# A fused Fourier mixing and gated feed-forward kernel: one row of the opening spread by TensorE, four small stores on another queue, one weight fold inside the loop

## The chip, the cores and the metric

The kernel runs on one core of a Trainium2 chip. A core has five engines with queues of their own: TensorE (PE, with its weight loads as PEld), VectorE (DVE), ScalarE (ACT), GpSimd (POOL) and SyncE (SP), which issues most DMAs. An engine works through its own queue strictly in order. The metric is the device time of one execution in microseconds; lower is better.

## The reference

```python
X = np.fft.fft(x, axis=1)          # x: 8 x 3008 x 256, float32
X = np.fft.fft(X, axis=2)
x = X.real.reshape(24064, 256)
h = x @ w_in                       # 256 x 2048
g = h * np.cos(h)
out = g @ w_out                    # 2048 x 256
```

Each of the 8 batches is transformed along its sequence and along its channels; the real part goes through a two-layer feed-forward block with the activation h*cos(h).

## The kernel before

**The transform.** The sequence length 3008 is 47 times 64, and the transform is done in two halves. `fold` adds and subtracts mirrored channels of the input tile `xp`; `first_half` multiplies a chunk (eight chunks per batch) by the small constant `L` into PSUM tile `pz`; ScalarE copies it to `zs`. `store_z` writes `zs` to DRAM and `load_z` reads it back transposed as `z2`, because the second half needs another partition order. `second_half(b, g)` multiplies `z2` by the constant `BJ` into `pb`, and ScalarE copies that to `pq`. One call makes one of six groups of a batch: 225 columns for group 0, 256 for the others.

**The channel transform is folded into the weights.** `fold_weights(e, n)` multiplies the 512-column quarter n of `w_in` by the cosine (e=0, to `WC`) or sine matrix (e=1, to `WS`): two matmul calls per quarter and side, four matmul records in the trace (`pw`), and a copy out of PSUM. One channel, the middle one, has no sine part, so row 0 of `WS` would be multiplied by zeros; that row of weights is sent out through DRAM by `send_wn`, and comes back as a column by `load_wn` (tile `wn`). The row of data that belongs to it is row 0 of the second part of `pq`; it must lie on all 128 partitions as the tile `nb`. `seed` (line 525) then starts each PSUM tile `H` on ScalarE with `wn * nb + 0.25`.

**How `nb` is made.** For all groups but the first of batch 0, SP stores that row to DRAM (`nd`, line 383), and when it has landed reads it back to 128 partitions (`nb`, line 384). For group 0 of batch 0 `spread_nb` does it on the chip: a matmul of a column of ones with the row (line 391, `pn`), and a ScalarE copy (line 392).

**The main loop.** A step is one group times one of eight blocks of the hidden width (two halves, `units`), so there are 8 x 6 x 8 steps and twice as many units k. Per unit, TensorE multiplies with `WC` and `WS` (`mm1`, line 544; before the second product ScalarE reads the first, `act_e`, line 556), VectorE mirrors (line 560), ScalarE rounds (572), VectorE takes the fraction (576), ScalarE takes the sine (582), VectorE multiplies (586), and GpSimd forms three sums per step (`sums`, lines 602, 608, 609). Seven products with the recombined second weights (`mm2`, line 635) follow five units later. Units 0 to 15 belong to group 0, units 16 to 31 to group 1. Unit 16 is seeded during unit 15; this is the first use of the second `nb`.

**What sets the order.** All queues' orders are written out by hand (a manual schedule). Ahead of the loop come the eight chunks of batch 0, with the stores of the first 4 of 24 column blocks (chunks 0 to 5 by SP, 6 and 7 by ScalarE's queue), the weight folds of quarters 0, 1 and 2, and `second_half(0, 0)`. Quarter 3 is folded inside the loop at k = 0 and 1. The other work of the opening (the remaining stores and loads of z, the recombination of the second weights by GpSimd in `combine_w2`, `second_half` for groups 1 to 5) hangs on the table `opening`, by step; `second_half(0, 1)` stands at step 4, that is after unit 9. The next batch's input loads `load_x(1, p)` stand at steps 0, 2, 4 and 6 on SP's queue.

**DMA semaphores.** The program gives every DMA one of eight semaphores, in the order in which the DMAs are planned to issue; a DMA waits until the one before it on the same semaphore has landed. So a DMA can be held by one that has nothing to do with its data, and on ScalarE's queue such a wait holds all ScalarE work behind it.

**PSUM.** Eight banks: four for the tag M (`pz`, `pw`, the accumulators of `mm2`) and four, H0 to H3, that the units use in turn. `borrow` takes the H bank that the next seed will use, and does not advance the turn.

Of the kernel before, what the change touches and what calls it, by code (L numbers as in the profile page):

```python
# [82 lines left out]
def _width(g):  # L83
    return 225 if g == 0 else 256
# [24 lines left out]
def kernel(  # L109
# [7 lines left out]
    nc = tc.nc  # L117
# [46 lines left out]
    def raw(q, i):  # L164
        return wl[:, 512 * i : 512 * i + 512] if q == 3 else wr[i][:, 512 * q : 512 * q + 512]
# [22 lines left out]
    def load_w2(f0, f1):  # L188
        nc.sync.dma_start(
            out=w2.rearrange("p (q c) -> p q c", c=ND)[:, 2 * f0 : 2 * f1],  # L190
            in_=moe_w_out.rearrange("(q p) c -> p q c", p=128)[:, 2 * f0 : 2 * f1],
        )
# [17 lines left out]
    def psum(name, tag="H"):  # L210
        at = tag
        if tag == "H":
            at = f"H{turn[0] % 4}"
            turn[0] += 1
        return ppool.tile([128, 512], FP, tag=at, bufs=bank[tag], name=name)

    def borrow(name, k=0):
        return ppool.tile([128, 512], FP, tag=f"H{(turn[0] + k) % 4}", bufs=1, name=name)
# [110 lines left out]
    def store_z(b, c, j0=0, j1=NJ, eng=nc.sync):  # L329
        half, q = divmod(c, NCH // 2)  # L330
        if q == 0 and j0 == 0:
            zds[b, half] = dpool.tile([32, 2 * NJ * 128], FP, tag="zd", bufs=4, name="zd")
        zd, zs = zds[b, half], zss[b, c]
        for e in range(2):
            p0 = 16 * e + IP * q
            eng.dma_start(
                out=zd[p0 : p0 + IP, 256 * j0 : 256 * j1].rearrange("i (y d) -> y i d", d=128),
                in_=zs[64 * e + 2 * j0 : 64 * e + 2 * j1, :].rearrange("y (i d) -> y i d", d=128),
            )
# [11 lines left out]
    ready = {}  # L351

    def second_half(b, g):

        T = _width(g)
        z2 = z2s[b]
        pb = borrow("pb") if b or g else psum("pb", "M")
        for q in range(4):
            jj = 4 * g + q
            nc.tensor.matmul(  # L360
                pb[:, 128 * q : 128 * q + 128],
                lhsT=z2[:, jj * 128 : jj * 128 + 128],
                rhs=BJ[:, jj * 128 : jj * 128 + 128],
                start=q == 0,
                stop=True,
                skip_group_check=True,
            )
        pq = spool.tile([128, 512], FP, tag="pq", bufs=8, name="pq")
        pv = pq[:, 0 : 2 * T].rearrange("d (e t) -> d e t", e=2)
        bv = pb.rearrange("d (q e k) -> d e q k", q=4, e=2)  # L370
        if g == 0:
            nc.scalar.copy(
                out=pv[:, :, 0:192].rearrange("d e (q k) -> d e q k", k=64), in_=bv[:, :, 1:4, :]
            )
            nc.scalar.copy(out=pv[:, :, 192:225], in_=bv[:, :, 0, 0:33])
        else:
            nc.scalar.copy(out=pv.rearrange("d e (q k) -> d e q k", k=64), in_=bv)
        nb = spool.tile([128, 256], FP, tag="nb", bufs=8, name="nb")
        ready[b, g] = (pq, nb)
        if b == 0 and g == 0:  # L380
            return
        nd = dpool.tile([1, 256], FP, tag="nd", bufs=4, name="nd")
        nc.sync.dma_start(out=nd[:, 0:T], in_=pq[0:1, T : 2 * T])
        nc.sync.dma_start(out=nb[:, 0:T], in_=nd[0:1, 0:T].to_broadcast([128, T]))


    def spread_nb():
        pq, nb = ready[0, 0]
        T = _width(0)
        pn = psum("pn", "M")  # L390
        nc.tensor.matmul(pn[:, 0:T], lhsT=ones, rhs=pq[0:1, T : 2 * T], start=True, stop=True)
        nc.scalar.copy(out=nb[:, 0:T], in_=pn[:, 0:T])

# [27 lines left out]
    def fold_weights(e, n, tag="M"):  # L421
        keep_weights(e, n, weights(e, n, tag))

    def weights(e, n, tag="M"):
        pw = psum("pw", tag)
        for i in range(2):
            nc.tensor.matmul(  # L427
                pw,
                lhsT=CS[i][:, 128 * e : 128 * e + 128],
                rhs=raw(n, i),  # L430
                start=(i == 0),
                stop=(i == 1),
            )
        return pw

    def keep_weights(e, n, pw, copy=nc.scalar.copy):
        W = WS if e else WC
        copy(out=W[:, 512 * n : 512 * n + 512], in_=pw)
# [26 lines left out]
    def send_wn(n):  # L465
        row = WS[0:1, 512 * n : 512 * n + 512]
        wds[n] = dpool.tile([1, 512], FP, tag="wd", bufs=3, name="wd")
        nc.scalar.dma_start(out=wds[n], in_=row)
        nc.gpsimd.memset(row, 0.0)
# [331 lines left out]
    first_half(0, 4)  # L801
    chunk(6)
    first_half(0, 5)
    store_z(0, 4, 0, 4)
    store_z(0, 5, 0, 4)
    load_z(0, 0, 0, 4)
    chunk(7)
    first_half(0, 6)
# [1 line left out]
    first_half(0, 7)  # L810
    store_z(0, 7, 0, 4, nc.scalar)
    load_z(0, 1, 0, 4)
    for n in (1, 2):
        fold_weights(1, n)
        send_wn(n)
        fold_weights(0, n)
    load_w2(0, 2)
    load_w(3)
    load_w2(2, 4)
# [5 lines left out]
    for half in range(2):  # L825
# [5 lines left out]
        0: ((combine_w2, 0, 2), (combine_w2, 2, 4)),  # L831
        3: ((combine_w2, 4, 6, 0, 2),),
        4: ((combine_w2, 4, 6, 2, 4), (second_half, 0, 1)),
        5: ((combine_w2, 6, 8, 0, 2),),
        6: ((combine_w2, 6, 8, 2, 4),),
        10: ((second_half, 0, 2), (load_ident,)),
        14: ((second_half, 0, 3),),
# [10 lines left out]
    n = len(steps)  # L848
# [16 lines left out]
    for k in range(2 * n + LAG):  # L865
        t, u = divmod(k, 2)
        d, v = divmod(k - LAG, 2)
        cur, prev, old, nxt = unit(k), unit(k - 1), unit(k - 2), unit(k + 1)
        done = step(d)
        full = step(d if v else d - 1, True)  # L870
        if cur:
            if k % (2 * per) == 0:
                todo = transform(cur.s.b + 1) if cur.s.b + 1 < NB else {}
            if k >= AHEAD:
                mm1(cur, 0)
                act_e(cur)
            if k == 0:
                for h in (cur, nxt):
                    mm1(h, 0)
                    seed_first(h)  # L880
                    act_e(h)
                spread_nb()
            if k < AHEAD - 1:
                mm1(cur, 1)
            if k == 0:
                pw = [weights(1, 3)]
        pair = None if u else pairs.pop(t, None)
        if pair:
            b, c = pair
            pz = [first_half(b, c, borrow("pz"))]  # L890
        if old:
            dve_g(old)
            if old.u:
                sums(old.s)
        if pair:
            pz.append(first_half(b, c + 1, borrow("pz", 1)))
        pm = clear_middle() if u and t in middles else None
        if done:
            order = (0, 1, 5, 4, 3, 2, 6) if done is steps[-1] else range(7)
            mm2(done, 4 * v, 4 * v + 3, order)  # L900
        if pm is not None:
            middle(pm)
        if full and full is not steps[-1]:
            take_m(full, 1 if v else 3, nc.vector)
        if nxt and 0 < k < AHEAD - 1:
            seed(nxt)
        if prev:
            act_round(prev)
        if pm is not None:
            nc.scalar.copy(out=zm[64:128], in_=pm)  # L910
        if pair:
            keep_z(b, c, pz[0])
        if nxt and k >= AHEAD - 1:
            seed(nxt)
        if full and full is not steps[-1]:
            take_m(full, 0 if v else 2, nc.scalar)
        if prev:
            dve_frac(prev)
        if k + 1 in range(2, AHEAD):
            mm1(nxt, 0)  # L920
            act_e(nxt)
        if k == 1:
            pw.append(weights(0, 3))
        copy_small()
        if prev:
            act_sin(prev)
        if pair:
            keep_z(b, c + 1, pz[1])
            patch_z(b, c)
            patch_z(b, c + 1)  # L930
        if cur and k >= AHEAD - 1:
            mm1(cur, 1)
        if done and v == 0:
            mm2(done, 3, 4, order)
        if cur:
            dve_h(cur)
        if k in (1, 2):
            keep_weights(2 - k, 3, pw[k - 1], nc.vector.tensor_copy)
        elif k == 3:
            send_wn(3)  # L940
        elif k == 6:
            load_wn(3, nc.scalar)
        if u == 0:
            continue
        for i in range(6):
            s = step(t - 4 - i, True)
            if s:
                combine_m(s, i)
        for sg, lag in ((0, 8), (1, 10)):
            s = step(t - lag, True)  # L950
            if s:
                store_out(s, sg)
        for call in opening.pop(t, ()):
            call[0](*call[1:])
        for call in todo.pop(t % per, ()):
            call[0](*call[1:])
# [31 lines left out]
```

## Time and profile before

| | |
|---|---|
| three runs, us | 1957.72, 1954.21, 1953.16 (median 1954.21) |
| the profiled execution, us | 1952.79 |
| its span from first to last instruction, us | 1951.0 |
| mean granted TensorE clock | 0.999 |
| TensorE busy | 1935.9 us, 9232 matmuls |
| ScalarE, VectorE, GpSimd busy | 1508.9, 1457.7, 1400.2 us |

Times in the profile count from the span's start. A row of the timeline gives start, duration, engine, line, operation and tiles, and in brackets how long the engine was idle before it and what ended the idle time. PEld is the weight load that goes ahead of each matmul; SPq and ACTq are DMA issues on those queues, and such a row shows the issue alone and not the transfer. Matmuls overlap, so the duration of a row is longer than the distance to the next; the distances between starts are what TensorE costs.

### The profile page before, as it was taken

The page shows a single profiled execution, that of the slowest core. Times are in us where ns is not written, and L with a number is a line of the kernel's source. Part 1 is how long each engine was busy: PE and PEld are TensorE (multiplying, and loading weights), DVE is VectorE, ACT ScalarE, POOL GpSimd, SP SyncE. Part 2 cuts the span into 40 slices and gives each one's busy share as a digit, 9 for nine tenths or more (in the row PEclk, how much of TensorE's full clock was granted, in tenths as well). Part 3 has the DMA queues.
Part 4 walks back from the last instruction along what each step waited for, and adds up shares of the span by engine and source line. Part 5 has one row for each costly group of instructions (what it writes and reads, how often), then busy time and mean ns, then how long its engine had stood idle before and what let it go on. Part 6 is the DMA issues. An engine that isn't in the chain of part 4 may idle for free.

```text
span 1951.0 us, 29624 instructions
## 1 busy us (share of the span) xinstructions
PE 1935.9 (99%) x9232; PEld 1682.9 (86%) x9232; DVE 1457.7 (75%) x2531; ACT 1508.9 (77%) x3444; POOL 1400.2 (72%) x1594
## 2 busy tenths in 40 slices
PE   8999999999999999999999999999999999999998
PEld 4888899888988889888898888988889888898887
DVE  3667777777777777777777777777777777778787
ACT  3777778777787777877778787787777887778775
POOL 3777767787677876787668776687767777666765
PEclk9999999999999999999999999999999999999999
DMA  7712024111230112301241111411124121110001
GB/s 184 141 27 44 20 47 84 24 36 33 53 71 18 40 40 59 54 20 40 43 78 31 32 34 41 86 24 39 24 42 84 24 40 28 39 22 16 11 14 31
DMA packets 178280, 88.71 MB, mean 45 GB/s; under 512 B 104890, under 2 KB 175209, under 8 KB 176492
## 3 DMA queue, kind: packets, MB, share of 16 engines
q1 hardware_dynamic: 176582, 86.35, 21.7%
q8 instruction: 75, 1.23, 0.3%
q14 instruction: 81, 0.66, 0.1%
q10 hardware_dynamic: 1542, 0.47, 0.1%
HBM read 49.51 MB, written 37.28 MB: 44 GB/s over the span
## 4 chain that ended last, share of the span: by engine, by line
PE 98%; DMA 1%; ACT 0%; DVE 0%; SPq 0%; issue 0%; POOL 0%; POOLq 0%; DVEq 0%
PE M L635 58%; PE H L544 33%; PE pz L269 3%; PE pb L360 2%; PE pw L427 1%; DMA xp<-in_x_dram 0%; DMA wr<-in_moe_w_in_dram 0%; DMA nb<-nd 0%; DMA nd<-pq 0%; PE pz L266 0%; PE pm L317 0%; DVE r L576 0%; DVE cb L703 0%; ACT r L582 0%; POOL xf L252 0%
## 5 line engine op out<-in xcount | busy, mean ns | idle before, releaser
L602 POOL TENSOR_TENSOR S<-r 128x512 f32<-128x512 f32 (+1 forms) x383 | 475.6, 1242 | 447.1 <-DVE r L586 398.5
L576 DVE SCALAR_TENSOR_TENSOR r<-r,H 128x512 f32<-128x512 f32 (+1 forms) x768 | 518.3, 675 | 195.5 <-ACT r L572 168.7
L582 ACT ACTIVATE r<-r 128x512 f32<-128x512 f32 (+1 forms) x768 | 477.0, 621 | 240.1 <-DVE r L576 235.2
L586 DVE SCALAR_TENSOR_TENSOR r<-H,r 128x512 f32<-128x512 f32 (+1 forms) x768 | 518.9, 676 | 133.8 <-ACT r L582 93.9
L635 PE MATMUL M<-S,VX 128*128 128x256 f32 (+1 forms) x2304 | 616.0, 376 | 0.0
L635 PEld LDWEIGHTS M<-S,VX 128*128 128x128 f32 x2304 | 436.0, 190 | 71.5 <-issue 22.7
L544 PE MATMUL H<-pq,WC 128*128 128x256 f32 (+1 forms) x1536 | 454.0, 377 | 3.9 <-ACT H L525 3.9
L544 PE MATMUL H<-pq,WS 128*128 128x256 f32 (+1 forms) x1536 | 451.1, 375 | 1.0 <-ACT ew L556 1.0
L572 ACT ACTIVATE r<-H 128x512 f32<-128x512 f32 (+1 forms) x768 | 447.7, 583 | 0.2 <-DVE H L560 0.2
L560 DVE TENSOR_TENSOR H<-ew,H 128x256 f32<-128x256 f32 (+1 forms) x768 | 324.7, 423 | 142.5 <-PE H L544 83.6
L635 PE MATMUL M<-r,w 128*128 128x256 f32 (+1 forms) x1536 | 387.6, 375 | 0.0
L556 ACT ACTIVATE ew<-H 128x256 f32<-128x256 f32 (+1 forms) x768 | 287.9, 375 | 121.5 <-PE H L544 117.0
L525 ACT ACTIVATE H<-nb,wn 128x256 f32<-128x256 f32 (+1 forms) x766 | 366.0, 478 | 4.9 <-DMA nb<-nd 4.0
L635 PEld LDWEIGHTS M<-r,w 128*128 128x128 f32 x1536 | 300.5, 196 | 26.9
L544 PEld LDWEIGHTS H<-pq,WC 128*128 128x128 f32 x1536 | 279.3, 190 | 48.3 <-ACT H L525 13.1
L544 PEld LDWEIGHTS H<-pq,WS 128*128 128x128 f32 x1536 | 290.0, 190 | 34.7 <-issue 1.6
L608 POOL TENSOR_TENSOR S<-S,r 128x256 f32<-128x256 f32 (+1 forms) x383 | 276.0, 721 | 30.0
L609 POOL TENSOR_TENSOR S<-r,S 128x256 f32<-128x256 f32 (+1 forms) x383 | 275.2, 718 | 30.0
L635 PE MATMUL M<-S,w 128*128 128x256 f32 (+1 forms) x768 | 225.5, 375 | 0.0
L635 PE MATMUL M<-r,VX 128*128 128x256 f32 (+1 forms) x768 | 225.2, 375 | 0.0
L635 PEld LDWEIGHTS M<-S,w 128*128 128x128 f32 x768 | 150.8, 197 | 14.6
L635 PEld LDWEIGHTS M<-r,VX 128*128 128x128 f32 x768 | 145.8, 190 | 14.6
(78 smaller groups left out, 918.1 us busy)
## 6 DMA issues: line engine op xcount, KB each, us to landing
out_dram<-ob SPq DMA_DIRECT2D x724, 32.0 KB
xp<-in_x_dram SPq DMA_DIRECT2D x56, 256.0 KB
zd<-zs SPq DMA_DIRECT2D x112, 96.0 KB
z<-zd SPq DMA_DIRECT2D x28, 384.0 KB
xp<-in_x_dram SPq DMA_DIRECT2D x56, 120.0 KB
nb<-nd SPq DMA_DIRECT2D x40, 128.0 KB
wr<-in_moe_w_in_dram SPq DMA_DIRECT2D x8, 256.0 KB
w<-in_moe_w_out_dram SPq DMA_DIRECT2D x4, 512.0 KB
```

The costliest lines, as they stand in the source:

```text
L525: nc.scalar.activation(out=h.H[:, 0:T], in_=s.nb[:, 0:T], func=AF.Copy, bias=0.25, scale=wn[:, f : f + 1])
L544: nc.tensor.matmul(h.H[:, 0:T], lhsT=W[:, 128 * f : 128 * f + 128], rhs=s.pq[:, e * T : e * T + T], start=False, stop=True, skip_group_che ...
L556: nc.scalar.mul(out=h.ew[:, 0:T], in_=h.H[:, 0:T], mul=2.0)
L560: nc.vector.tensor_tensor(out=h.H[:, T : 2 * T][:, ::-1], in0=h.ew[:, 0:T], in1=h.H[:, 0:T], op=ALU.subtract)
L572: nc.scalar.activation(out=r, in_=y, func=AF.Copy, bias=BIG, scale=1.0)
L576: nc.vector.scalar_tensor_tensor(out=r, in0=r, scalar=-BIG, in1=y, op0=ALU.add, op1=ALU.subtract)
L582: nc.scalar.activation(out=r, in_=r, func=AF.Sin, bias=0.0, scale=SIN_SCALE)
L586: nc.vector.scalar_tensor_tensor(out=r, in0=y, scalar=-0.25, in1=r, op0=ALU.add, op1=ALU.mult)
L602: tt(out=sv[:, 0:2], in0=qv[:, 1:2].to_broadcast([128, 2, T]), in1=qv[:, 0:4:3], op=ALU.subtract,)
L608: tt(out=sv[:, 2], in0=sv[:, 1], in1=gv[:, 0, 0], op=ALU.subtract)
L609: tt(out=sv[:, 3], in0=gv[:, 1, 0], in1=sv[:, 2], op=ALU.add)
L635: nc.tensor.matmul(acc[key][m // 2][:, 256 * (m % 2) : 256 * (m % 2) + T], lhsT=w, rhs=a, start=first, stop=s.fp == 7, skip_group_check=True,)
```

## The change

Three things are moved in the opening of the kernel; nothing is changed from batch 1 on.

1. Group 1 of batch 0 gets its `nb` from `spread_nb(1)` instead of the two DMAs. It stands in `opening` at step 5 (after unit 11), and takes its PSUM tile by `borrow`.
2. The stores of chunks 4 and 5 (two DMAs each, first 4 column blocks) are issued by ScalarE's queue instead of SP's.
3. `fold_weights(0, 2)` is no longer done before `second_half(0, 0)`. Its matmuls come at k = 2 in the loop, after quarter 3's, and its copy out of PSUM is done by VectorE at k = 3.

```diff
-        if b == 0 and g == 0:
+        if b == 0 and g < 2:
             return
         nd = dpool.tile([1, 256], FP, tag="nd", bufs=4, name="nd")
         nc.sync.dma_start(out=nd[:, 0:T], in_=pq[0:1, T : 2 * T])
         nc.sync.dma_start(out=nb[:, 0:T], in_=nd[0:1, 0:T].to_broadcast([128, T]))
 
-    def spread_nb():
-        pq, nb = ready[0, 0]
-        T = _width(0)
-        pn = psum("pn", "M")
+    def spread_nb(g):
+        pq, nb = ready[0, g]
+        T = _width(g)
+        pn = borrow("pn") if g else psum("pn", "M")
         nc.tensor.matmul(pn[:, 0:T], lhsT=ones, rhs=pq[0:1, T : 2 * T], start=True, stop=True)
         nc.scalar.copy(out=nb[:, 0:T], in_=pn[:, 0:T])
...
     first_half(0, 5)
-    store_z(0, 4, 0, 4)
-    store_z(0, 5, 0, 4)
+    store_z(0, 4, 0, 4, nc.scalar)
+    store_z(0, 5, 0, 4, nc.scalar)
     load_z(0, 0, 0, 4)
...
-    for n in (1, 2):
-        fold_weights(1, n)
-        send_wn(n)
-        fold_weights(0, n)
+    fold_weights(1, 1)
+    send_wn(1)
+    fold_weights(0, 1)
+    fold_weights(1, 2)
+    send_wn(2)
...
-        5: ((combine_w2, 6, 8, 0, 2),),
+        5: ((combine_w2, 6, 8, 0, 2), (spread_nb, 1)),
...
-                spread_nb()
+                spread_nb(0)
...
-        if k == 1:
-            pw.append(weights(0, 3))
+        if k in (1, 2):
+            pw.append(weights(0, 4 - k))
...
-        if k in (1, 2):
-            keep_weights(2 - k, 3, pw[k - 1], nc.vector.tensor_copy)
-        elif k == 3:
+        if k in (1, 2, 3):
+            e, q = ((1, 3), (0, 3), (0, 2))[k - 1]
+            keep_weights(e, q, pw[k - 1], nc.vector.tensor_copy)
+        if k == 3:
             send_wn(3)
```

## The prediction

> **What bounds the kernel now.** I read the page first, then the chain of waits over the opening, then waits and stages around its longest break, because the change touches the opening alone.
>
> ```profile
> span 1951.0 us, 29624 instructions
> ...
> PE 98%; DMA 1%; ACT 0%; DVE 0%; SPq 0%; issue 0%; POOL 0%; POOLq 0%; DVEq 0%
> ```
>
> TensorE is on the chain for 98% of the span, so a gain is either TensorE work removed or TensorE idle time removed. The change removes no matmul (it adds two records, below); it can gain only in the part that is not TensorE. The chain shows where that is:
>
> ```profile
> 68.11 2.89 DMA nd<-pq
> 71.01 4.16 DMA nb<-nd
> 75.19 0.49 ACT H L525
> 75.72 1.22 PE H L544 x2
> ```
>
> ```profile
> ACT H L525 <- DMA nb<-nd: 4.0, 1, 4.0
> PE H L544 <- ACT H L525: 3.5, 1, 3.5
> ```
>
> The columns of the chain are start, duration, what. The two DMAs take 7.05 us; ScalarE idles 4.0 us for the second before it can seed unit 16, and TensorE 3.5 us behind it. The stages show a second loss: TensorE restarts at a lower granted clock (1.00 in every 4 us stage from 20 to 72).
>
> ```profile
> 72.00:76.00 4.00, 0.52 (x3) 0.28 (x2) 0.30 (x1) 0.81 (x2) 3.84 (x5) 0.93 0.87 147
> 76.00:80.00 4.00, 4.00 (x14) 3.53 (x15) 1.70 (x4) 2.16 (x8) 1.43 (x2) 0.64 1.06 159
> ```
>
> Columns: stage, busy time of PE, PEld, DVE, ACT, POOL, then clock, DMA share, GB/s. The clock is 0.64 in the 4 us after the idle stage.
>
> **Part 1: the row spread by TensorE.** What the wait costs is read from three equal places of the TensorE timeline, the first `WC` product of units 13, 15 and 17:
>
> ```profile
> 65.61 0.54 PE L544 MATMUL H<-pq,WC 128*128 128x225 f32 x2
> ...
> 69.80 0.54 PE L544 MATMUL H<-pq,WC 128*128 128x225 f32 x2
> ...
> 79.36 0.59 PE L544 MATMUL H<-pq,WC 128*128 128x256 f32 x2
> ```
>
> Two undisturbed units take 69.80-65.61 = 4.19 us, the two with the wait 79.36-69.80 = 9.56. The difference is 5.37, less 0.1 for the two products of unit 16 that are 256 instead of 225 columns wide (0.54 against 0.59 us in these rows): **5.27 us**, of which 3.5 are idle and 1.8 the slower matmuls. The lower bound is 3.5, if the low clock had another cause and stayed; I take 5.27, because no other stage shows it. The Trainium skill, "TensorE: Matmul & The Clock Gate", Part 1, says that an idle window of about 3.4 us drops the clock to half and that about 3.4 us of work restores it; this trace agrees (3.5 idle, 0.64 after).
>
> In its place come two matmul records and one ScalarE copy. Their price, and whether they wait:
>
> ```profile
> 38.02 0.38 PE pn L391 x2
> ...
> 62.23 0.62 DVE L586 SCALAR_TENSOR_TENSOR r<-H,r 128x450 f32<-128x450 f32 x1 [0.28 <-ACT r L582]
> ...
> 63.71 0.54 PE L544 MATMUL H<-pq,WC 128*128 128x225 f32 x2
> ...
> 60.00:64.00 4.00, 4.00 (x22) 3.83 (x22) 2.62 (x5) 3.30 (x9) 3.77 (x6) 1.00 1.06 302
> ```
>
> The 225-column spread cost TensorE 0.38 us; 256 columns make 0.38*256/225 = 0.43. It goes ahead of unit 12's `WC` product at 63.71. The borrowed bank was unit 9's, last read by the VectorE row that ends at 62.85, so TensorE does not wait for it. TensorE is busy 4.00 of 4.00 there, so 0.43 is paid in full. The copy sits behind unit 10's sine on ScalarE, which has 0.70 us free in that stage against about 0.4; behind it are unit 12's `act_e` and unit 13's seed, and both wait for TensorE's 0.43 anyway. Its result is wanted three units later: hidden. SP loses two issues, and the four loads that stood behind `nb` on its queue go some 3 us earlier (from behind 71.01 to about 68.1). Part 1: 0.43-5.27 = **-4.84**.
>
> **Part 2: stores by ScalarE's queue, and the fold taken out.** They go together: the fold hides the arrival of z.
>
> ```profile
> 21.86 8.08 SPq L336 DMA_DIRECT2D zd<-zs  x12
> 30.11 1.87 SPq L346 DMA_DIRECT2D z<-zd  x4
> 32.51 3.79 SPq L177 DMA_DIRECT2D wr<-in_moe_w_in_dram  x2
> ...
> 25.48 1.08 SPq L336 DMA_DIRECT2D zd<-zs  x2
> ```
>
> ```profile
> SPq L177 <- DMA wd<-WS: 2.9, 1, 2.9
> SPq L336 <- DMA wr<-in_moe_w_in_dram: 1.9, 2, 1.0
> ```
>
> ```profile
> 25.58 0.59 ACT L295 COPY zs<-pz 128x512 f32<-128x512 f32 x1 [2.01 <-PE pz L283]
> ...
> 27.75 0.63 ACTq L336 DMA_DIRECT2D zd<-zs  x2
> ```
>
> ```profile
> 26.67 7.13 PE L427 MATMUL pw<-wr,CS 128*128 128x512 f32 x16
> ...
> 33.67 0.97 PEld L360 LDWEIGHTS pb<-BJ,z 128*128 128x128 f32 x8 [0.70 <-issue]
> ...
> 39.73 0.30 PEld L427 LDWEIGHTS pw<-wr,CS 128*128 128x128 f32 x2 [0.72 <-DMA wr<-in_moe_w_in_dram]
> ...
> 28.00:32.00 4.00, 4.00 (x11) 1.79 (x10) 0.00 (x0) 1.17 (x2) 0.52 (x1) 1.00 0.28 61
> ```
>
> Sixteen fold records run from 26.67; at 0.43 each, four less end 1.72 us sooner, near 31.95. But the weight load of `pb` starts at 33.67 after 0.70 us, so z lands about then, some 2 us after SP's last of four issues (30.11+1.87 = 31.98, its start near 31.6). With z unmoved nothing is gained. SP now issues eight stores instead of twelve. The fourth store can't leave before 25.48 (held by a weight load, 1.9 us in two such waits); the last then leaves near 27.0, lands near 28.5 (I estimate 1.5 us for the landing of a store: before, the last of the twelve leaves near 29.65 and the third z load, which needs it, near 31.2, in the middle of its row), and the loads of the first half follow. Those of the second half need chunk 7's store, which ScalarE issues at 27.75 to 28.38; I add 0.2 for its four more issues (0.3 each, inside the 2.01 us idle before 25.58, except that the last is held by the same weight load until about 25.9). Landing 1.5 later, the last load leaves near 30.4 instead of 31.6: z comes **1.2 us** sooner (bounds: 0, if another landing holds it; 1.72, the fold). ScalarE's later copies wait for TensorE in any case. The DMA share of 0.28 says that the transfers have room.
>
> A side effect: SP's second load of quarter 3 was held 2.9 us by a landing of `wd` only because both used one semaphore. In the new order its predecessor is a z load that has landed by then, so quarter 3 arrives up to 2.9 us earlier, and TensorE, there 1.2 us sooner, doesn't wait for it (0.72 before).
>
> **Part 3: the fold put in at k = 2.**
>
> ```profile
> 41.62 1.72 PE pw L427 x4
> ...
> 44.54 0.65 PE L544 MATMUL H<-pq,WS 128*128 128x225 f32 x2 [0.45 <-ACT ew L556]
> 45.35 0.65 PE L544 MATMUL H<-pq,WC 128*128 128x225 f32 x2 [0.16 <-ACT H L525]
> ...
> 46.54 0.62 PE L544 MATMUL H<-pq,WS 128*128 128x225 f32 x2 [0.54 <-ACT ew L556]
> 47.42 0.65 PE L544 MATMUL H<-pq,WC 128*128 128x225 f32 x2 [0.27 <-ACT H L525]
> ...
> 46.03 0.36 ACT L556 ACTIVATE ew<-H 128x225 f32<-128x225 f32 x1 [0.27 <-PE H L544]
> ```
>
> It costs 1.72 us on TensorE, in front of four waits of 0.45+0.16+0.54+0.27 = 1.42. So the bounds are 0.30 and 1.72. Followed through: the product at 44.54 moves to 45.8 and the next, now without wait, to 46.2; it ends near 46.7, so the `act_e` at 46.03 starts 0.7 later, and all that hangs on it on ScalarE (sine, seed) with it: 47.42 becomes about 48.07. I take **+0.65**. VectorE's copy (0.7 us as its two neighbours) comes after the mirror of unit 3, where VectorE waits for ScalarE's late sine.
>
> **The sum.** -4.84-1.2+0.65 = **-5.4**. Against the profiled execution (1952.79 = span 1951.0 and 1.8 around it) that is 1947.4; the median of the runs lies 1.4 above that execution, and I forecast on its level: 1954.21-5.4 = **1948.8 us**. About 0.2% (3.9 us) is what can be told from no change.
>
> **The rivals.**
>
> *Nothing is gained ahead of the loop.* Z lands no sooner and the fold is paid in full at k = 2: 0+1.72-4.84 = -3.1, 1951.1. For it: ScalarE's DMAs use the same semaphores and can be held by the same weight loads. Against it: SP's twelve issues take 8.08 us at a DMA share of 0.28. The Trainium skill, "DMA: Bandwidth & Descriptors", section "Issuing engines are not separate DMA queues", speaks for this rival: all queues end on the same 16 engines, and a second issuing engine saves only issue time. No row here separates the two.
>
> *GpSimd takes the place of the removed wait.*
>
> ```profile
> 73.67 1.06 POOL L602 TENSOR_TENSOR S<-r 128x450 f32<-128x450 f32 x1
> ...
> 81.36 0.54 PE L635 MATMUL M<-S,VX 128*128 128x225 f32 x2
> ```
>
> Its sums of step 6 started at 73.67, while TensorE stood, and are first used at 81.36; 5.4 us sooner that is 75.96, against 74.73, when they are there. The margin is 1.2 us; GpSimd was busy 3.77 and 3.84 of 4.00 us around there. Were its queue 3 us later (its recombinations wait for loads of the second weights), TensorE would lose 1.8: 1950.6. Against it: those loads move forward with SP's queue.
>
> *Slower: ScalarE is held by a DMA semaphore.* Its send and load of quarter 3's row take new semaphores, and now follow other stores.
>
> ```profile
> 52.34 0.40 ACTq L472 DMA_DIRECT2D wn<-wd  x1
> ...
> SPq L150 <- DMA wn<-wd: 4.3, 1, 4.3
> ...
> 59.30 0.32 SPq L150 DMA_DIRECT2D xp<-in_x_dram  x1
> ```
>
> A DMA of this stretch can be in flight from 52.34 to 59.30, 7 us. If ScalarE had to wait for one as long, TensorE would stand about 7 us and restart slowly (1.8 as above): -5.4+7+1.8 = +3.4, 1957.6. It decides from a hold of 3.6 us with the slow restart. Against it: both follow stores issued some 5 us before, as they did.
>
> **How the numbers follow.** Forecast 0.70 (its own range 1947.3 to 1950.4: the bounds of z's arrival and of part 3), nothing gained ahead of the loop 0.15, GpSimd 0.08, ScalarE held 0.07. Two in ten are left out by 1946.5 to 1953.0, where the two middle rivals lie with the runs' spread. Faster by over 0.2% (below 1950.3): nearly all of the forecast and a part of the middle two, 0.73. Slower by over 0.2% is ScalarE held, with a part of it inside the bound and other unseen holds, 0.07. Within 0.2%: 0.20.
>
> **What would show it.** Right: no wait of line 525 for `nb` near 70 us and a clock of 1.00 there; `pb`'s first weight load near 32.5; the first product behind the new fold follows without idle time; unit 17's `WC` product near 73.9 instead of 79.36. Wrong: TensorE idle time in front of `pb` as long as the fold that left, an idle ScalarE behind one of its DMA issues, or products with `S` that wait for GpSimd.

## The result, and the profile after

The changed kernel takes 1947.69 us (median of 7 executions, 1947.33 to 1948.46); the kernel before, run beside it, 1954.21 us (7 executions, 1952.76 to 1958.42). The ratio is 0.9959 with a 95% interval of 0.9949 to 0.9970: faster by 0.4%, or 8.0 us (5.9 to 10.0). The medians alone differ by 6.5 us, the two profiled executions by 5.5 (1952.79 and 1947.33). Forecast were -5.4 us and 1948.8 us. The three measured differences do not agree, because the executions of before spread over 5.7 us and those of the changed kernel over 1.1; what spreads them is half of this study.

The page of the changed kernel:

```profile
span 1945.5 us, 29626 instructions
...
PE 98%; DMA 1%; SPq 0%; DVE 0%; issue 0%; ACT 0%; DVEq 0%
```

The same stages as in the prediction (duration, busy time of PE, PEld, DVE, ACT, POOL, clock, DMA share, GB/s), and the new product of the changed kernel with the first `WC` products of units 15 and 17, which answer to the rows at 69.80 and 79.36:

```profile
72.00:76.00 4.00, 4.00 (x22) 3.77 (x21) 3.05 (x6) 3.29 (x11) 3.84 (x6) 1.00 1.10 169
76.00:80.00 4.00, 4.00 (x22) 3.71 (x21) 3.06 (x6) 3.60 (x9) 2.34 (x4) 1.00 0.89 150
```

```profile
62.61 0.69 PE L391 MATMUL pn<-pq,ones 1*128 1x256 f32 x2
...
69.43 0.54 PE L544 MATMUL H<-pq,WC 128*128 128x225 f32 x2
...
73.72 0.59 PE L544 MATMUL H<-pq,WC 128*128 128x256 f32 x2
```

TensorE is busy 4.00 of 4.00 in both stages, the clock is 1.00, and unit 17's first product comes at 73.72 instead of 79.36.

The gain can be cut into stretches that begin where TensorE starts a row that both kernels have: the first fold record, and the three first calls of `second_half`. After (and, behind it, the two rows of before that the prediction did not show):

```profile
26.26 5.42 PE L427 MATMUL pw<-wr,CS 128*128 128x512 f32 x12
32.27 1.13 PE L360 MATMUL pb<-BJ,z 128*128 128x128 f32 x8 [0.59 <-DMA z<-zd]
...
57.36 1.05 PE L360 MATMUL pb<-BJ,z 128*128 128x128 f32 x8
...
85.14 1.05 PE L360 MATMUL pb<-BJ,z 128*128 128x128 f32 x8
```

```profile
58.56 1.05 PE L360 MATMUL pb<-BJ,z 128*128 128x128 f32 x8
...
90.78 1.05 PE L360 MATMUL pb<-BJ,z 128*128 128x128 f32 x8
```

Every kernel below is cut the same way, each in its own profiled execution, in us. The first `pb` of before starts at 33.70.

| kernel | first fold | fold to 1st pb | 1st to 2nd pb | 2nd to 3rd pb | to the span's end |
|---|---|---|---|---|---|
| before | 26.67 | 7.03 | 24.86 | 32.22 | 1860.2 |
| changed | 26.26 | 6.01 | 25.09 | 27.78 | 1860.4 |
| row_only | 27.46 | 7.27 | 24.69 | 27.77 | 1860.0 |
| row_and_stores | 27.77 | 6.97 | 24.61 | 27.92 | 1859.9 |
| row_and_fold | 27.69 | 7.22 | 25.09 | 28.74 | 1860.4 |
| stores_fold_only | 26.83 | 5.95 | 25.09 | 34.79 | 1860.5 |
| before_again | 27.38 | 7.13 | 25.90 | 36.48 | 1860.2 |
| wait_kept_warm | 27.11 | 7.18 | 24.69 | 30.64 | 1860.2 |
| before_bj_late | 27.32 | 7.21 | 24.70 | 28.01 | 1860.3 |
| before_bj_early | 26.23 | 7.11 | 24.82 | 33.75 | 1860.2 |
| after_bj_late | 27.81 | 5.92 | 25.09 | 27.78 | 1860.4 |
| before_wn_on_chip | 27.00 | 7.16 | 24.84 | 30.35 | 1860.0 |
| after_wn_on_chip | 27.44 | 6.14 | 25.42 | 27.77 | 1860.4 |

The last column is the same in all to 0.6 us: whatever any edit does happens before the third `pb`. The first column does not go by the edits: it lies between 26.26 and 27.81 in the kernels with the stores moved and between 26.23 and 27.69 in the others. I take it for chance between executions, 0.41 us of it in favour of the changed kernel's profile. What the edits do is in the three columns between.

### The profile page after: what moved, and what is told of

Same layout as the page of the kernel before. It is cut to its first block, busy times and chain, and to the rows that moved or that the text cites. A ratio compares the mean times of both kernels' runs of the same rounds, so it can differ in the third digit from the quotient of the medians.

```text
span 1945.5 us, 29626 instructions
## 1 busy us (share of the span) xinstructions
PE 1933.3 (99%) x9234; PEld 1681.4 (86%) x9234; DVE 1459.1 (75%) x2532; ACT 1508.3 (78%) x3444; POOL 1400.4 (72%) x1594
## 4 chain that ended last, share of the span: by engine, by line
PE 98%; DMA 1%; SPq 0%; DVE 0%; issue 0%; ACT 0%; DVEq 0%
PE M L635 59%; PE H L544 34%; PE pz L269 3%; PE pb L360 2%; DMA xp<-in_x_dram 1%; DMA wr<-in_moe_w_in_dram 0%; PE pw L427 0%; DMA zd<-zs 0%; PE pz L266 0%; PE pm L317 0%; DMA z<-zd 0%; DVE cb L703 0%; SPq L147 0%; PE H L531 0%; PE po L733 0%
```

## The experiments

All medians are of the runs that the ratio compares; each group of kernels was timed beside executions of before of its own (medians 1955.85 for row_only, stores_fold_only, wait_kept_warm and before_again; 1956.66 for row_and_fold, before_bj_late, before_bj_early and after_bj_late; 1954.29 for row_and_stores, before_wn_on_chip and after_wn_on_chip).

### Which part does what

**row_only**: part 1 of the change alone.

```diff
-        if b == 0 and g == 0:
+        if b == 0 and g < 2:
...
-        5: ((combine_w2, 6, 8, 0, 2),),
+        5: ((combine_w2, 6, 8, 0, 2), (spread_nb, 1)),
```

> The kernel before with part 1 alone: the second group's row is spread by TensorE; stores and fold stay as they were. Theory (the forecast's step): the wait of 5.27 us goes and 0.43 comes, so about 4.8 us under the profiled execution of before, near 1948.0; since the executions of before lie between 1952.8 and 1958.4 and those of the changed kernel between 1947.3 and 1948.5, I expect the spread of before to go with this part too, and the ratio near 0.996. Rival (the spread comes from the opening ahead of the loop): near 1948 with single executions 4 to 5 us above.

Measured: 1948.96 us, ratio 0.9967 (0.9955 to 0.9980). Part 1 brings most of the gain. Its effect is all in the stretch from the second to the third `pb`: 32.22 becomes 27.77, that is -4.45. The executions lie between 1948.07 and 1951.25: narrower than before's but not as narrow as the changed kernel's.

**stores_fold_only**: parts 2 and 3 alone (the changed kernel with the row again through DRAM).

```diff
-        if b == 0 and g < 2:
+        if b == 0 and g == 0:
...
-        5: ((combine_w2, 6, 8, 0, 2), (spread_nb, 1)),
+        5: ((combine_w2, 6, 8, 0, 2),),
```

> The changed kernel without part 1: stores 4 and 5 on ScalarE's queue and the fold at k = 2, but the second group's row again through DRAM. Theory A (the terms simply add): -0.8 us against before, near 1952, with before's spread. Theory B (the row's two DMAs stand on SyncE's queue behind input loads, and the second of these waits for the landing of the weight row's column wn, which in the changed kernel's trace lands at 62.4 instead of 59.3): the row lands some 3 us later, TensorE waits about 7 us and more instead of 3.5, and the kernel is 1 to 4 us slower than the fast executions of before, near 1954 to 1957.

Measured: 1955.75 us, ratio 0.9998 (0.9989 to 1.0007): no gain. The opening is 1.1 us shorter (5.95 against 7.03), and the stretch with the wait 2.6 us longer (34.79). Its chain of waits shows why; the columns are start, duration, what:

```profile
51.65 11.87 DMA wn<-wd
...
67.65 5.02 DMA nd<-pq
72.68 4.21 DMA nb<-nd
```

The column `wn` is 11.87 us in flight here, SyncE's input loads wait for it, and the row stands behind those. Theory B expected this order of events and executions near 1954 to 1957; they lie between 1953.2 and 1957.4. Against before as a whole there is no loss, because before has such executions too (before_again, below).

**row_and_fold** and **row_and_stores**: part 1 with the fold but not the stores, and with the stores but not the fold.

```diff
-    store_z(0, 4, 0, 4, nc.scalar)
-    store_z(0, 5, 0, 4, nc.scalar)
+    store_z(0, 4, 0, 4)
+    store_z(0, 5, 0, 4)
```

```diff
 # row_only, and:
-    store_z(0, 4, 0, 4)
-    store_z(0, 5, 0, 4)
+    store_z(0, 4, 0, 4, nc.scalar)
+    store_z(0, 5, 0, 4, nc.scalar)
```

> The changed kernel with the stores of chunks 4 and 5 back on SyncE's queue (parts 1 and 3 together). The forecast's terms: z lands as before (pb's weight load at 33.7), the fold costs its 0.65 at k = 2 and is not paid back, so the kernel is some 1.2 to 1.4 us slower than the changed kernel, near 1949.0, and equal to or slower than part 1 alone (1948.96). Rival (the skill's rule, stores gain only issue time; z's arrival is set by something else): equal to the changed kernel, 1947.7, with pb as early as there (32.3).

> Parts 1 and 2 without the fold: stores 4 and 5 on ScalarE's queue, all folds ahead of the loop. The forecast's step (z's arrival and the fold hide each other): pb starts when the 16 fold records end, some 7.0 us after they begin, as before, against 6.0 in the changed kernel; no gain ahead of the loop, near 1948.8. In the stretch from there to the second pb it should be 24.7 us like part 1 alone, against 25.1 with the fold at k = 2.

Measured: 1950.10 us (ratio 0.9968, 0.9959 to 0.9977) and 1949.13 us (0.9972, 0.9961 to 0.9984). Both are what part 1 gives alone, and the opening says the same with less chance in it: 7.22 and 6.97 us from the first fold to the first `pb`, against 6.01 with both. With the fold moved and the stores left, TensorE only waits for z instead of folding (waits of row_and_fold, total, count, longest):

```profile
PE pb L360 <- DMA z<-zd: 1.8, 1, 1.8
```

So neither gains without the other: 1.0 to 1.2 us as a pair, less the 0.2 to 0.5 that the fold costs in the loop (24.6 to 24.9 without it, 25.09 with it, in every kernel of the table but two: before_again, where the granted clock falls to 0.58 from 48 to 52 us, and after_wn_on_chip, which has more work in it). What is left of the pair, under 1 us, is read from the traces; the times do not show it, since the interval of the changed kernel overlaps that of row_only.

### What the wait costs

**wait_kept_warm**: seven products of 128x256, used by nothing, ahead of unit 16's first product.

```diff
+    def fill(k):
+        pd = borrow("pd")
+        for i in range(k):
+            nc.tensor.matmul(
+                pd[:, 0:256], lhsT=VX[:, 0:128], rhs=VX[:, 0:256], start=i == 0, stop=i == k - 1
+            )
...
+        7: ((fill, 7),),
```

> The kernel before with 7 extra products of 128x256 on TensorE ahead of unit 16's first product, into the PSUM bank that unit 17 takes next; they are used by nothing. Theory (1.8 us of the wait's cost is the granted clock after an idle stretch): TensorE idles 0.5 us instead of 3.5, the clock stays at 1.00 and the time falls by about 1.8 us although 3 us of work are added. Rival (the slow stretch behind the wait has another cause): no gain. On the spread: if it is the clock's, it goes; if it is the row's landing, single executions stay 4 us and more above the others.

Measured: 1951.80 us, ratio 0.9990 (0.9980 to 1.0000): about 2 us faster with more work, though the interval reaches no change. The trace is clearer. Its TensorE rows and stages:

```profile
76.09 0.70 PE L551 MATMUL H<-pq,WC 128*128 128x256 f32 x2 [0.40 <-ACT H L532]
...
72.00:76.00 4.00, 3.69 (x18) 2.98 (x16) 0.70 (x2) 0.44 (x2) 3.84 (x6) 1.00 0.78 142
76.00:80.00 4.00, 3.91 (x20) 3.67 (x21) 2.56 (x5) 3.61 (x11) 2.75 (x4) 1.00 1.06 156
```

The clock stays at 1.00 and the stretch is 30.64 instead of 32.22, with the row landing at the same place (16.6 us behind the second `pb` in both): the slower matmuls behind the wait are the clock's, 1.6 us here. The executions still spread from 1950.99 to 1959.82, so the spread is not the clock's alone.

**before_again**: the kernel before, unchanged.

> The kernel before, unchanged, for a second profile and more executions. If its executions fall into two groups again (near 1953 and near 1958), Theory B expects that a slow one shows wn landing 3 us and more later than 59.3 and the seed of unit 16 waiting that much longer than 4.0 us; a rival (the clock alone) expects the same landings and a longer stretch under 1.00.

Measured: executions from 1951.95 to 1958.88, not two clean groups but a broad spread; ratio 0.9996 (0.9986 to 1.0005), as it should be. The profiled one is the longest, 1958.88 us. Its chain and stages:

```profile
54.17 12.84 DMA wn<-wd
...
71.14 5.11 DMA nd<-pq
...
76.27 4.54 DMA nb<-nd
```

```profile
76.00:80.00 4.00, 0.18 (x1) 0.00 (x0) 0.23 (x1) 0.00 (x0) 3.84 (x5) 0.83 0.56 92
80.00:84.00 4.00, 2.64 (x7) 2.31 (x8) 1.16 (x2) 2.36 (x7) 0.09 (x1) 0.50 1.16 162
```

```profile
ACT H L525 <- DMA nb<-nd: 5.7, 1, 5.7
```

This is the same kernel as the one in the prediction. `wn` is 12.84 us in flight instead of 7 and lands at 67.0 instead of 59.3; the row lands at 80.8 instead of 75.2; ScalarE waits 5.7 us instead of 4.0, and the clock is at 0.50 for the next whole stage. The stretch takes 36.48 us instead of 32.22. Theory B is right for this execution, but not all of the 4.26 us is the wait that the change removes. TensorE is held up twice, first because unit 12's seed waits for `wn` itself, then for the row. The rows for both waits, and the first `WC` products of units 15 and 17 (73.74 and 85.47):

```profile
67.54 0.65 PE L544 MATMUL H<-pq,WC 128*128 128x225 f32 x2 [1.81 <-ACT H L525]
...
73.74 0.54 PE L544 MATMUL H<-pq,WC 128*128 128x225 f32 x2
...
81.36 1.22 PE L544 MATMUL H<-pq,WC 128*128 128x256 f32 x2 [5.18 <-ACT H L525]
...
85.47 0.60 PE L544 MATMUL H<-pq,WC 128*128 128x256 f32 x2
```

In the changed kernel unit 15's product and unit 17's are 73.72-69.43 = 4.29 us apart. Here they are 11.73 apart, in the prediction's trace 9.56. So the wait for the row cost 7.44 us in this execution and 5.27 in the one on which the forecast was made, 2.17 more; the other 2.09 us lie ahead of unit 13, nearly all of them where the seed waits for `wn`. The change does not take this wait for `wn` away: in row_and_fold, with `wn` 12.52 us in flight, it still idles TensorE for 0.89 us.

The clock has a part as well. It also falls at a place that has nothing to do with the row:

```profile
48.07 1.12 PE L544 MATMUL H<-pq,WC 128*128 128x225 f32 x2 [0.27 <-ACT H L525]
```

This product takes 1.12 us, in the kernel before's first profile 0.65 (47.42), with the same idle pieces of 0.45, 0.16, 0.54 and 0.27 us in front of it; the stages say 0.58 from 48 to 52 us here and 1.00 there. From this row to the second `pb` it is 12.34 us against 11.14. What makes the clock fall here is not shown.

### Why the row is late

The packets of the two queues, in one microsecond of each kernel: first before, 57 to 58 us, then before_again, 62 to 63. q1 is SyncE's queue and q10 ScalarE's, whose packets there are `wn`'s 4-byte ones; columns are packets, MB, share of 16 engines.

```profile
q1 hardware_dynamic: 295, 0.29, 96.2%
q10 hardware_dynamic: 346, 0.00, 19.5%
```

```profile
q1 hardware_dynamic: 61, 0.41, 104.0%
q10 hardware_dynamic: 33, 0.00, 2.1%
```

In the first, the small packets go by beside packets of 1 KB on average; in the second only some tens per microsecond pass, beside packets of 6.7 KB on average (the 1 MB load of BJ has rows of 8 KB). The late landings of the changed kernel, stores_fold_only and row_and_fold show such microseconds too. That suggested the BJ load as the culprit. It can't be the whole of it: in the last microsecond before `wn` lands in before_again, 66 to 67 us, its packets pass still more slowly, with next to nothing beside them:

```profile
q10 hardware_dynamic: 7, 0.00, 0.4%
q1 hardware_dynamic: 1, 0.00, 0.1%
```

**before_bj_late** and **before_bj_early**: before with the BJ load behind step 5, and one place up.

```diff
-    load_bj(1024, NJ * 128)
...
-        5: ((combine_w2, 6, 8, 0, 2),),
+        5: ((combine_w2, 6, 8, 0, 2), (load_bj, 1024, NJ * 128)),
```

```diff
+    load_bj(1024, NJ * 128)
     load_w2(6, 8)
-    load_bj(1024, NJ * 128)
```

> The kernel before with the 1 MB load of BJ moved on SyncE's queue from ahead of the next batch's inputs to behind step 5; nothing else. Theory B (the weight row's column wn is carried in 4-byte packets; where the BJ load is issued ahead of it or with it, its packets alternate with BJ's 8 KB packets and it lands at 62 to 67 instead of 59; SyncE's next input load waits for it, and the second group's row stands behind those): wn lands before 59 in every execution, the row lands near 68 to 70, before ScalarE wants it at 71, the wait of 4.0 us goes without any spread by TensorE, and the executions lie together within 1.5 us, near 1948 to 1949. Rival (the row's DMAs are slow by themselves, 7 us whatever is queued ahead): the wait stays at 3 us or more, above 1951.

> The kernel before with the BJ load moved up by one place, ahead of the last load of the second weights, so that it is always issued ahead of wn's load. Theory B: wn always lands late (62 to 67), every execution is like the slow ones of before, 1956 to 1959, with no execution below 1955. Rival (the slow executions of before come from the clock or from the start, not from the order of these two loads): the spread of before, 1952 to 1958, unchanged.

Measured: late, 1949.95 us, ratio 0.9971 (0.9961 to 0.9981). Moving one load that has nothing to do with the row gets most of part 1's gain. The wait is not gone, but it is 1.3 us (TensorE 0.8), the clock stays at 1.00 in all stages from 20 us on, and the stretch is 28.01:

```profile
ACT H L525 <- DMA nb<-nd: 1.3, 1, 1.3
```

Much of the expectation missed all the same. `wn` was in flight about 7.1 us (issued at 53.01; SyncE's load that waits for it leaves at 60.14), so it did not land before 59, and the executions lie between 1947.93 and 1952.22, not within 1.5 us. The row came sooner in this profile without an earlier `wn`: its first DMA leaves at 66.06, 6.8 us behind the second `pb`, where it was 9.6 us behind it before (68.11), and the 1 MB is issued behind the row instead of ahead of it.

Early, 1954.35 us, ratio 0.9996 (0.9984 to 1.0007): no change, and executions from 1951.44 to 1958.05. Theory B's expectation missed here: with BJ always issued ahead of `wn`, `wn` was 7.00 us in flight in the profiled execution, not 11 and more:

```profile
51.95 7.00 DMA wn<-wd
...
72.00:76.00 4.00, 0.00 (x0) 0.00 (x0) 0.00 (x0) 0.42 (x2) 3.84 (x6) 0.74 0.84 138
76.00:80.00 4.00, 3.90 (x10) 3.39 (x11) 1.25 (x2) 2.54 (x8) 1.14 (x1) 0.50 1.05 149
```

So which of the two was issued first does not decide how long `wn` flies. That the large load delays the row is shown by the time of before_bj_late; that it does so through `wn` is not shown by this profile, and the rule by which an execution comes out short or long is not known.

**before_wn_on_chip**: `wn`'s quarter 3 by TensorE, so that its packets are gone.

```diff
         elif k == 3:
-            send_wn(3)
-        elif k == 6:
-            load_wn(3, nc.scalar)
+            take_wn(3)
```

> The kernel before with quarter 3's row of weights turned into its column by TensorE at k = 3 (four tiny products and a copy, as for quarter 0) instead of by the two DMAs on ScalarE's queue; the 4-byte packets are gone. Theory (the slow executions are those in which these packets alternate with 8 KB packets, with idle DMA engines after them): SyncE's input loads start near 55 in every execution, the row's wait stays between 2 and 4.5 us because the DMA engines are busy until about 70 in any case, and the executions lie near 1952 to 1954.5 with none above 1956. Rival (the slow executions come from elsewhere): the spread of before, 1951 to 1959, stays.

Measured: 1952.03 us, ratio 0.9988 (0.9978 to 0.9997); 11 executions from 1950.43 to 1954.94, none above 1956, where 6 of the 16 executions of before beside it and 17 of the 30 beside before_bj_late lie. The long executions go with these packets. Without the BJ load beside the packets there are none either (before_bj_late, none above 1952.22), so it takes both. What stays is the wait of the short ones:

```profile
ACT H L525 <- DMA nb<-nd: 3.6, 1, 3.6
...
72.00:76.00 4.00, 0.87 (x5) 0.52 (x4) 0.72 (x2) 0.71 (x2) 3.82 (x5) 1.00 0.83 153
76.00:80.00 4.00, 4.00 (x21) 3.74 (x22) 2.84 (x5) 3.40 (x10) 2.44 (x3) 1.00 1.04 152
```

TensorE idles 3.1 us there and the clock does not drop. The stretch is 30.35.

### What is left in the changed kernel

The changed kernel's seed of unit 12 waits for `wn`, too:

```profile
62.47 0.45 ACT L525 ACTIVATE H<-nb,wn 128x225 f32<-128x225 f32 x1 [0.78 <-DMA wn<-wd]
```

**after_bj_late** and **after_wn_on_chip** take that wait of the seed away, by the same two edits on the changed kernel.

```diff
-    load_bj(1024, NJ * 128)
...
-        5: ((combine_w2, 6, 8, 0, 2), (spread_nb, 1)),
+        5: ((combine_w2, 6, 8, 0, 2), (spread_nb, 1), (load_bj, 1024, NJ * 128)),
```

```diff
         if k == 3:
-            send_wn(3)
-        elif k == 6:
-            load_wn(3, nc.scalar)
+            take_wn(3)
```

> The changed kernel with the BJ load moved behind step 5. Theory B: the seed of unit 12 no longer waits 0.8 us for wn, which lands before 59; 0.3 to 0.4 us of TensorE time come back, near 1947.2, and SyncE's input loads start at 57 to 59 instead of 62.5. Rival: 0.8 us of wait on the seed is hidden by other work: no difference from the changed kernel (1947.7).

> The changed kernel with the same replacement. The row's wait is gone already, so nothing waits long for that column: the four tiny products cost about 0.5 us at k = 3, where TensorE idles 0.5 us in the changed kernel, and I expect 0 to +0.5 us against the changed kernel, 1947.5 to 1948.5. Rival (late input loads still cost something later): faster than the changed kernel by more than 0.5 us.

Measured: 1948.55 us (0.9965, 0.9952 to 0.9978) and 1948.45 us (0.9964, 0.9952 to 0.9977). Both intervals overlap the changed kernel's. The table settles it: the seed's wait for `wn` is gone in both, the stretch is 27.78 and 27.77 against 27.78, so the 0.78 us on ScalarE cost TensorE nothing, as the rival had it. In after_bj_late `wn` landed at about 61.3 and not before 59, 8.7 us after its issue although the BJ load was out of its way; the four tiny products cost 0.3 us (25.42 against 25.09). Neither beats the changed kernel.

## Why the prediction was right or wrong

**The mechanisms of the three parts were right in the main; the step that failed is the last of the sum: "the median of the runs lies 1.4 above that execution, and I forecast on its level".** It takes the saving of one profiled execution for the saving of any, as if what lifts the other executions above it had nothing to do with the wait. By the prediction's own measure, unit 15's product to unit 17's, the wait cost 5.27 us in that execution, 7.44 in before_again and 80.22-69.41-4.29 = 6.52 in before_bj_early. The changed kernel has no such wait, so most of the lift goes with it: by the ratio -8.0 us (5.9 to 10.0) instead of -5.4. The median, 1947.69, still lies in the stated range, but 8.0 us below the level of 1954.21 would be 1946.2, under the range. The spread stood in the times (1953.16 to 1957.72), and the row that hinted at its cause was quoted in the third rival: a DMA that flies 7 us and holds SyncE.

Not all of the spread is traced. Kernels that have part 1 and a late `wn` keep some of it (row_and_fold up to 1952.56), and the clock falls in places of its own (before_again).

**The sum against the profiled execution.** It said 1947.4, and the changed kernel's profiled execution took 1947.33. That closeness is partly luck. The three columns of the table give -1.02+0.23-4.44 = -5.23; the savings of parts 1 and 2 were put too high by 0.4 and 0.2 and the cost of part 3 too high by 0.4; and 0.41 us of the 5.5 is the earlier start. The forecast's own range, 1947.3 to 1950.4, does not come out of the bounds that it names, either: z from 0 to 1.72 and part 3 from 0.30 to 1.72 give 1948.0 to 1951.1.

**Part 1, 5.27 out and 0.43 in.** The 5.27 is right for the profiled execution (9.56-4.29, above). The stretch is 32.22-27.77 = 4.45 shorter, so the spread costs 0.82, not 0.43. The row before it, which was 0.38 us from unit 12's `WC` product (63.33 to 63.71, the first row below), is 1.09 us from it (62.14 to 63.23) in the changed kernel:

```profile
63.33 0.54 PE L635 MATMUL M<-S,VX 128*128 128x225 f32 x2
```

```profile
62.14 0.54 PE L635 MATMUL M<-S,VX 128*128 128x225 f32 x2
...
62.61 0.29 PEld L391 LDWEIGHTS pn<-pq,ones 1*128 1x128 f32 x2 [0.28 <-DVE r L576]
```

That is 0.71, and the way to the next `WC` product is 0.11 longer. The same distances stand in row_only, where `wn` came in time. "TensorE does not wait for it" was wrong: the profile puts the wait of the new weight load down to VectorE. Whether the borrowed bank is the reason is not shown; the VectorE row that the prediction named as its last reader had ended at 61.67.

Of the 5.27, 3.48 are idle. The 1.8 given to the clock were 1.6 (wait_kept_warm); before_wn_on_chip, with the clock at 1.00, pays 3.39 us by the same measure for 3.13 of idle time, so some 0.3 of a restart is not the clock's. The rule of the Trainium skill, "TensorE: Matmul & The Clock Gate", Part 1, an idle window of about 3.4 us, fits this wait in every profile: idle stretches of 0.8 and 3.1 us left the clock at 1.00, those of 3.5 us and more did not. No idle window of that length stands in front of the fall at 48 us in before_again, only idle pieces of at most 0.54 us; so the clock here falls without such a window, too, and by the measurement the rule is not the whole of it.

**Part 2, -1.2 (0 to -1.72).** Right, and for the reason given: 7.03 becomes 6.01, that is -1.0. ScalarE's four issues were held as estimated ("until about 25.9"):

```profile
22.72 3.21 ACTq L336 DMA_DIRECT2D zd<-zs  x4
```

They end at 25.93. That stores and fold "go together" is shown by the two kernels that have one of them. Of the side effect on quarter 3, the earlier load holds: SyncE's two issues of it end at 32.08 instead of 36.30. No wait of its product for `wr` is left, but that is no proof, since row_only has none either.

**Part 3, +0.65 (0.30 to 1.72).** Too dear. Against before it is 25.09-24.86 = +0.23, below the lower bound. But before's 24.86 holds the wait for quarter 3 (0.72 us on the weight load). row_only, which has neither that wait nor the fold in the loop, takes 24.69, so the fold itself costs about +0.4, inside the bounds. The prediction named that wait as a side effect but did not put it into the same balance.

**The rivals.** Nothing gained ahead of the loop: refuted (6.01 against 7.03). With it goes the reading of the Trainium skill, "DMA: Bandwidth & Descriptors", section "Issuing engines are not separate DMA queues", by which the stores would not land sooner. The section grants a second issuing engine the saved issue time, and here that was enough: SyncE's eight stores took 5.84 us to issue where twelve had taken 8.08. GpSimd: its sums do not hold TensorE (no such wait in the changed kernel near 75 us). ScalarE held by a DMA semaphore: it came, in a small form and at another place than was feared. Behind its four store issues ScalarE idles until an earlier store has landed:

```profile
25.96 0.59 ACT L295 COPY zs<-pz 128x512 f32<-128x512 f32 x1 [2.73 <-DMA zd<-zs]
```

Before, it idled 2.01 us at this place for TensorE. Chunk 7's store leaves 1.60 us behind the first fold instead of 1.08, and z still comes 1.0 us sooner. The DMA that the rival named, `wn`, holds SyncE's queue and not ScalarE's. Its landing makes the row late where the row goes through DRAM; in the changed kernel's profile it costs TensorE nothing.

**Open.** What makes `wn` fly 7 or 12 us in executions of one and the same kernel. The kernel before, row_only, wait_kept_warm and before_bj_early profiled short (7.0 to 7.7), before_again long (12.8); the changed kernel, stores_fold_only, row_and_fold and row_and_stores are all long (11.3 to 12.5). The order of issue alone is excluded by before_bj_early. Also open is what makes the clock fall without a long idle stretch, and how much of the spread that is: most executions of before above 1956 us have a mean granted clock of 0.995 to 0.998, but some, 1958.26 us among them, have 0.999.

## What to carry to other kernels

A profile is one execution. Where the executions of a kernel spread by as much as the change is worth (here 5.7 us against 5.4), the wait that the change removes may differ between them, and the saving is its mean, not its value in the one trace. Cut the profiles of several executions at rows they share; here the first 97 us held all of the spread, most of it in one stretch of 30 us, and the remaining 1860 us agreed to 0.6. Two edits that hide each other (a fold in front of a load, and the load's earlier start) have to be judged as a pair, since either alone gains nothing.

## What was not expected of the hardware

A load of 512 packets of 4 bytes, 2 KB in all, took between 7.0 and 12.8 us to land, and with the next input load waiting for its landing it held SyncE's queue for 4.3 to 11.1 us. In the changed kernel the two queues stood still meanwhile (62 to 63 us: no packet on either). Moving an unrelated 1 MB load out of that stretch was worth 0.29% (0.19 to 0.39).

An idle stretch of 3.1 us cost TensorE 3.4 us, one of 3.5 cost 5.3, and one of 5.2 cost 7.4, with the clock at 0.50 from 80 to 84 us. In the last of these executions the clock was also at 0.58 from 48 to 52 us, without an idle piece above 0.54 us in front of it.
